# Router logits of the last two token tiles from running sums and eight extra columns of the last second weights, with split second weights kept in DRAM

## Chip, cores and metric

The kernel runs on one core of a Trainium2 chip. The metric is the device time of one execution in microseconds (us), median of three. Below, TensorE, VectorE, ScalarE, GpSimd and SyncE are the engines that the profile calls PE (its weight loads PEld), DVE, ACT, POOL and SP. SyncE issues almost all transfers, from one queue in program order.

## What is computed

Three layers in a row on 1536 tokens (2 sequences of 768) of 512 features. The first is linear attention with a decay, in blocks of 64 tokens. The other two are:

```python
p = domain_probs / (domain_probs.sum(-1, keepdims=True) + 1e-09)   # layer 2, 4 experts, dense
for e in range(4):
    out += p[:, e:e + 1] * (np.maximum(x @ w1[e], 0.0) @ w2[e])    # 512 -> 1024 -> 512
...
logits = x @ w_gate                                                # layer 3, 8 experts, one per token
expert_idx = np.argmax(logits, axis=1)
gate_w = softmax(logits)[expert_idx]
out[mask_e] = gate_w[mask_e, None] * (np.maximum(x[mask_e] @ w1[e], 0.0) @ w2[e])
```

All values are fp32. A product is made of three passes over values split into a high part (`fp32r`) and the rest: high by high, low by high, high by low.

## The kernel before

**Attention and the first pass.** Twelve chunks of 128 tokens go through attention; `warmup` (L1095) runs 54 matmuls on ones ahead of it, `att_a` (L453) multiplies the scores of a chunk by the decays on VectorE, one operation for each half of the heads. The first dense half-expert is worked in between.

**The dense layer.** Tokens come in two sweeps of 768 (6 tiles of 128 each); each sweep goes through 8 half-experts k (512 hidden units). `FAST` passes (k = 1 to 13, `fast_unit`, L714) make the first product of a half-expert in 14 block products ("b phase", line L740, tiles `b`) and then the second product tile by tile ("y phase", `moe1_mm2`, L621, tiles `y`), whose result VectorE adds into `acc` (L636). `hook1(i)` follows block product i, `hook2(j)` follows tile j of the y phase; through them the splits of the next weights (`split_plain`, L184: a copy to the high part on ScalarE, L208, and a subtraction on VectorE, L210) and the router's work are put in order by hand. `KEPT` passes (k = 8 to 13, the second sweep) do not split the first weights `w0` again: the first sweep wrote the parts to DRAM (`kept`, L218), and `kept_steps` loads them. The second weights `w1` are loaded raw and split in every pass. The last dense expert (k = 14 and 15 together, both halves) is done at the end of the sweep, 256 tokens at a time: eight `h` products, then `y` for two tiles. After the f-th `h` of the i-th 256 tokens comes hook 10 i + f, after their tiles hooks 10 i + 8 and 10 i + 9; `plan` lists what is done there.

**The router.** Logits of tiles 0 to 8 are made on VectorE, one operation for each tile and expert (`logit_v`, L845, a product with a row of the router's weights and a sum over 512 values; a ring of five rows is in SBUF). Tiles 9, 10 and 11 use TensorE: four transposes (`route_x`, L853) and a product with the router's weights (`route_lg`, L865). `route_choose` (L875) finds the largest logit (VectorE: `mx`, `sc`, `m2`, `oh` one after the other, and `df`, `seen`), `route_rank` (L915) counts on TensorE how many tokens came before (it reads `oh`), `route_send` makes the row number and scatters the token's row to the expert's bin in DRAM (`scatter`, on GpSimd).

**The end of the dense layer.** The last tiles y = 10 and z = 11 set when the third layer can start. Tile 10 is summed by `moe1_mm2`; tile 11 by `last_dense` (L646) in two halves of 256 columns, each in two runs of 12 matmuls. The transposes and logits of both tiles come between. The first expert's bin is read back (`first_load`, tile `xe`) without the last two tiles; their tokens are put in by a product with a selection matrix (`first_sel`, `first_place`, parts from `first_parts`), on top of the transposed `xe` (`first_T`) in two PSUM banks, two tiles `px` in each. `rows_split` makes the parts `xg` of it, and the products `g` of the first expert begin. `last_sends` scatters the last two tiles; `load_rows` of the first two experts waits for all scatters, and the weights owed to the third layer are loaded behind it.

```python
    y, z = NC - 2, NC - 1
    at(20, route_x, c + 1)          # c + 1 is tile 9, c is tile 8
    at(21, route_choose, c + 1)
    at(23, route_choose, c)
    at(23, route_send, c + 1)
    at(25, route_send, c)
```

Of the kernel before, what the change touches and what calls it, by code (L numbers as in the profile page):

```python
# [18 lines left out]
P = 128  # L19
# [58 lines left out]
def body(ctx: ExitStack, tc: tile.TileContext, lam, att, dp, w1a, w2a, wg, wgt, w1b, w2b, out):  # L78
# [29 lines left out]
    lg_v = const.tile([P, VT, E2], F32, name="lg_v")  # L108
# [32 lines left out]
    loads = [(w, k) for w, k in blocks if w or k not in KEPT]  # L141
    wt = {}
    raws = [rawp]
# [40 lines left out]
    def split_plain(n, c, only=""):  # L184
        b = blocks[n]
        k = b[1]
        if c == 0 and only != "l":
            wt[b] = tuple(
                wp.tile([P, 4, HF], F32R, tag=f"w{b[0]}{x}", name=f"w{b[0]}{x}_{b[1]}")
                for x in "hl"  # L190
            )
        if b in EARLY_AT and c < EARLY:
# [27 lines left out]
    }  # L220

# [231 lines left out]
    def att_a(c):  # L453
# [7 lines left out]
        for r in range(2):  # L461
            V.tensor_tensor(out=a[r], in0=qk[r], in1=w[:, r], op=ALU.mult)
# [179 lines left out]
    def last_parts(hs, j, c, i):  # L642
        return [
            ((hh[:, j * P:j * P + P], hl[:, j * P:j * P + P]),
             tuple(w[:, f % FC, c] for w in wt[1, KL - 1 + f // FC]))
# [3 lines left out]
    def last_dense(hs, t0, j, m, i):  # L649
        t = t0 // P + j  # L650
        c = slice(m * HD, m * HD + HD)
        if i == 0:
            rt["yz"] = ps_mm.tile([P, 512], F32, tag="mm", name=f"yz{m}")[:, :HD]
        ps = rt["yz"]
        mm3(ps, last_parts(hs, j, c, i), i == 0, i == 1)
        if i == 1:
            e = half(KL) // 2
            V.scalar_tensor_tensor(
                out=acc[:, t, c], in0=ps, scalar=p_sb[:, t, e:e + 1], in1=acc[:, t, c],
                op0=ALU.mult, op1=ALU.add,  # L660
            )

# [125 lines left out]
    def open_routing():  # L788
        op = ctx.enter_context(pool("order", 1, side="right"))
        for name, n, d in (  # L790
            ("places", EN, F32), ("caps", EN, F32), ("count", E2, F32), ("place", EN, F32),
            ("cap_e", E2, F32), ("nth", EN, I32), ("tmp", E2 * max(OMAX, E2), F32),
# [59 lines left out]

    def route_x(t, ds=range(KD)):  # L853
# [21 lines left out]
    def route_choose(t):  # L875
        rp = rt["rs"]
        if t < VT:
# [80 lines left out]
    def last_sends():  # L958
# [17 lines left out]
        V.tensor_scalar(  # L976
# [3 lines left out]
        V.tensor_scalar(  # L980
# [3 lines left out]
        V.tensor_tensor(out=at_row, in0=at_row, in1=far, op=ALU.add)  # L984
        V.tensor_tensor(out=pos, in0=at_row, in1=rk_all[:, two], op=ALU.add)
        V.tensor_scalar(out=sums, in0=sums, scalar1=1e-9, scalar2=None, op0=ALU.add)
        V.reciprocal(acc[:, two, DM], sums)
        for i in range(n):
            t = NC - n + i
            scatter(bins, pos[:, i:i + 1], acc[:, t, :], E2 * MOST, "bins")  # L990
# [10 lines left out]
    def first_T(s):  # L1001
        if s == 0:
            px = [ps_mm.tile([P, 512], F32, tag="mm", name=f"px{d}") for d in range(2)]
            rt["px"] = [px[d // 2][:, d % 2 * CAP:d % 2 * CAP + CAP] for d in range(KD)]
        for d in range(KD):
# [860 lines left out]
```

## Time and profile before

| | |
|---|---|
| median of 3 runs | 739.46 us (738.38 to 740.17) |
| the profiled execution's own time | 739.93 us |
| its span, first to last instruction | 738.1 us |
| PE busy | 727.1 us, 99% of the span |
| DVE busy | 510.9 us, 69% |
| ACT busy | 313.7 us, 42% |
| POOL busy | 81.2 us, 11% |
| mean granted TensorE clock | 0.997 |

The span is the stretch in which instructions run; the time is 1.8 us longer. Matmuls are pipelined and the profile models their ends, so a matmul's own duration is longer than its share of the engine, which is the distance between two starts.

### The profile page before, as it was taken

What the parts mean: (1) busy time and instruction counts of PE and PEld (TensorE: products, weight loads), DVE (VectorE), ACT (ScalarE), POOL (GpSimd) and SP (SyncE); (2) the same over time, 40 slices, a digit from 0 to 9 for tenths busy, and PEclk for the clock granted to TensorE, in tenths of its full rate; (3) what the DMA queues carried; (4) which work ended last, traced back from release to release, by engine and by line L of the source; (5) the groups of instructions that cost most, each with busy time, mean ns of one, the idle gap of its engine ahead of it and who ended that gap; (6) DMA issues with size and microseconds to landing.
All of it is one profiled execution on the core that took longest, in us unless ns stands there. A gap on an engine that the chain in (4) does not pass through costs nothing.

```text
span 738.1 us, 12981 instructions
## 1 busy us (share of the span) xinstructions
PE 727.1 (99%) x4951; PEld 658.9 (89%) x4951; DVE 510.9 (69%) x1140; ACT 313.7 (42%) x690; POOL 81.2 (11%) x86
## 2 busy tenths in 40 slices
PE   9999999999999999999999999999999999999995
PEld 8888989889898988989889898988898998998994
DVE  7557776776756766657677667774696867675883
ACT  4333725243342535424223141541153757565772
POOL 3474000000000000000000002100021013121013
PEclk9999999999999999999999999999999999999998
DMA  8763794626446175455161543361143968765661
GB/s 315 286 217 104 249 262 175 256 93 255 158 180 256 58 284 229 155 202 212 59 257 38 218 156 145 100 200 39 52 113 133 323 222 270 255 209 187 229 231 32
DMA packets 39420, 136.79 MB, mean 185 GB/s; under 512 B 6913, under 2 KB 6913, under 8 KB 34747
## 3 DMA queue, kind: packets, MB, share of 16 engines
q1 hardware_dynamic: 37243, 129.63, 50.6%
q0 software_dynamic: 2112, 6.31, 2.2%
q8 instruction: 40, 0.66, 0.4%
q14 instruction: 25, 0.20, 0.1%
HBM read 102.85 MB, written 33.26 MB: 184 GB/s over the span
## 4 chain that ended last, share of the span: by engine, by line
PE 96%; DVE 1%; ACT 1%; issue 1%; POOL 0%; POOLq 0%; DVEq 0%
PE y L595 36%; PE b L740 26%; PE h L595 7%; PE g L595 5%; PE z L595 3%; PE z L1479 3%; PE g L1479 2%; PE zr L1588 2%; PE qk L395 1%; PE z L1480 1%; PE g L1480 1%; PE xo L529 1%; PE zr L1559 1%; PE warm L1098 1%; PE yz L595 1%; PE gr L595 1%
## 5 line engine op out<-in xcount | busy, mean ns | idle before, releaser
L210 DVE TENSOR_TENSOR w1l<-raw,w1h 128x512 fp32r<-128x512 f32 x124 | 82.4, 688 | 28.5 <-ACT w1h L208 28.1
L636 DVE SCALAR_TENSOR_TENSOR acc<-y,p_sb,acc 128x512 f32<-128x512 f32 x77 | 57.8, 751 | 61.2 <-PE y L595 54.2
L747 ACT COPY u<-b 128x384 f32<-128x384 f32 x78 | 36.4, 479 | 108.6 <-PE b L740 107.1
L208 ACT CAST w1h<-raw 128x512 fp32r<-128x512 f32 x124 | 73.1, 619 | 1.1 <-DMA raw<-in_w2a 1.1
L125 POOL DMA_INDIRECT bins<-acc,pos x10 | 11.2, 1117 | 456.9 <-DVE mx L889 378.5
L740 PE MATMUL b<-xh,w0h 128*128 128x384 f32 x208 | 57.8, 339 | 0.0
L210 DVE TENSOR_TENSOR w0l<-raw,w0h 128x512 fp32r<-128x512 f32 x76 | 51.2, 722 | 0.8 <-ACT w0h L208 0.6
L846 DVE CUSTOM_DVE_ANT_0 x<-acc,x 128x512 f32<-128x512 f32 x72 | 49.4, 687 | 1.0
L208 ACT CAST w0h<-raw 128x512 fp32r<-128x512 f32 x76 | 42.9, 623 | 4.5 <-DMA raw<-in_w1a 4.0
L125 POOL DMA_INDIRECT out<-y,xb x16 | 30.0, 1878 | 132.6 <-DVE y L1625 82.8
L754 DVE TENSOR_TENSOR u<-b,u 128x384 f32<-128x384 f32 x78 | 43.1, 552 | 1.4 <-PE b L740 1.4
L740 PEld LDWEIGHTS b<-xh,w0h 128*128 128x128 f32 x208 | 38.2, 188 | 0.6
L595 PE MATMUL g<-xg,w0h 128*128 128x288 f32 (+1 forms) x192 | 38.1, 294 | 0.0
L595 PE MATMUL h<-xh,w0h 128*128 128x256 f32 x144 | 36.0, 292 | 0.2 <-ACT xh L181 0.2
L740 PE MATMUL b<-xl,w0h 128*128 128x384 f32 x104 | 35.2, 339 | 0.0
L595 PE MATMUL h<-xh,w0l 128*128 128x256 f32 x144 | 34.7, 282 | 0.1
L740 PE MATMUL b<-t1h,w0h 128*128 128x384 f32 x104 | 30.8, 337 | 0.0
L595 PEld LDWEIGHTS g<-xg,w0h 128*128 128x128 f32 x192 | 30.8, 188 | 0.0
L740 PE MATMUL b<-xh,w0l 128*128 128x384 f32 x104 | 28.8, 338 | 0.0
L740 PE MATMUL b<-t4h,w0l 128*128 128x384 f32 x104 | 28.8, 337 | 0.0
L740 PE MATMUL b<-t2h,w0l 128*128 128x384 f32 x104 | 28.7, 337 | 0.0
L740 PE MATMUL b<-t3h,w0h 128*128 128x384 f32 x104 | 28.6, 336 | 0.0
(371 smaller groups left out, 2053.6 us busy)
## 6 DMA issues: line engine op xcount, KB each, us to landing
raw<-in_w2a SPq DMA_DIRECT2D x32, 512.0 KB, 3.5
raw<-in_w1b SPq DMA_DIRECT2D x32, 512.0 KB, 5.7
raw<-in_w2b SPq DMA_DIRECT2D x32, 512.0 KB, 4.4
kept<-w0h SPq DMA_DIRECT2D x12, 1024.0 KB, 7.9
w0h<-kept SPq DMA_DIRECT2D x12, 1024.0 KB, 9.5
raw<-in_w1a SPq DMA_DIRECT2D x18, 512.0 KB, 3.7
att<-in_att SPq DMA_DIRECT2D x12, 512.0 KB, 4.7
kept<-w0l SPq DMA_DIRECT2D x6, 1024.0 KB, 6.6
```

The costliest lines, as they stand in the source:

```text
L125: i = G.indirect_dma_start(out=dst, out_offset=bass.IndirectOffsetOnAxis(ap=idx, axis=0), in_=src, in_offset=None, bounds_check=rows - 1, ...
L208: A.copy(out=hi, in_=t)
L210: V.tensor_tensor(out=lo, in0=t, in1=hi.bitcast(F32), op=ALU.subtract)
L595: T.matmul(ps, l, r, start=first and i == 0, stop=last and i == len(ops) - 1)
L636: V.scalar_tensor_tensor(out=acc[:, t, 0:DM], in0=ps, scalar=p_sb[:, t, e:e + 1], in1=acc[:, t, 0:DM], op0=ALU.mult, op1=ALU.add,)
L740: T.matmul(ps, l[:, d, c], r[:, d, :], start=first and i == 0, stop=i == len(ops) - 1, skip_group_check=not first,)
L747: A.copy(out=t, in_=bank[2, s])
L754: V.tensor_tensor(out=t, in0=bank[b, s], in1=t, op=ALU.add)
L846: V.tensor_tensor_reduce(out=x2.rearrange("p d t -> p (d t)")[:, RING * DM:], in0=acc[:, t, 0:DM], in1=logit_piece(e), scale=1.0, scalar=0 ...
L1479: T.matmul(ps[:, :2 * n], wh, both, start=i == 0, stop=False)
L1480: T.matmul(ps[:, :n], wl, hi, start=False, stop=i == len(parts) - 1)
L1588: T.matmul(ps[s][:st], l[:, c], r, start=h == 0 and j == 0, stop=h == 1 and j == len(ops) - 1)
```

## The change

Four things are changed together.

1. The logits of tiles 10 and 11. In the passes k = 10 to 13 VectorE makes, for each of the last dense expert's 1024 rows of second weights, its eight products with the router's rows (`wg_v`, 64 operations on rows loaded anew by `wg_load`, 24 loads of 256 KB); `wg_columns` splits these and puts them behind the 512 columns of the second weights as eight more. `logit_v` is done for tiles 10 and 11 on the sums without the last dense expert, and `last_dense` adds the rest: its right half has 264 columns, and one small VectorE operation adds the last eight to the logits. The transposes and logit products of tiles 10 and 11 go away, and so does `keep_up`.
2. Second weights in the second sweep. In the first sweep the split second weights of passes 2 to 7 are written to DRAM (2 MB each), and passes 8 to 13 load the two parts (`fetch_second`) and split nothing. The order of the router's operations in these passes is denser (`logit`).
3. The end of the dense layer is put in another order: both last tiles by `last_dense`, right half first; tile 8 and 9 are sent one hook earlier; four small operations of `last_sends` move from VectorE to GpSimd; `px` has a bank for each of its four tiles; raw loads of the third layer stand behind `first_load` and not ahead of it.
4. The start: 46 warming matmuls and not 54, and `att_a` of the first two chunks in halves.

```diff
-    loads = [(w, k) for w, k in blocks if w or k not in KEPT]
+    loads = [(w, k) for w, k in blocks if k not in KEPT]
     wt = {}
+    wx = {}
...
+        if c == 3 and b[0] and k < KS and k in kept:
+            for i, t in enumerate(wt[b]):
+                SP.dma_start(out=kept2[k][i], in_=t.bitcast(F32))
...
+    kept2 = {k: dram.tile([2, P, 4, HF], F32, name=f"kept2_{k}") for k in kept}
+    def fetch_second(n, i):
+        k = blocks[n][1]
+        t = wp.tile([P, 4, HF + E2], F32R, tag="w1" + "hl"[i], name=f"w1{'hl'[i]}_{k}")
+        t = t[:, :, :HF]
+        SP.dma_start(out=t.bitcast(F32), in_=kept2[half(k)][i])
+        wt[1, k] = wt.get((1, k), ()) + (t,)
     def pair_of(t, j):
...
-        for r in range(2):
-            V.tensor_tensor(out=a[r], in0=qk[r], in1=w[:, r], op=ALU.mult)
+        step = HP // 2 if c < B else HP
+        for h in range(0, HP, step):
+            for r in range(2):
+                i = slice(h, h + step)
+                V.tensor_tensor(out=a[r][:, i], in0=qk[r][:, i], in1=w[:, r, i], op=ALU.mult)
...
     def last_parts(hs, j, c, i):
         return [
             ((hh[:, j * P:j * P + P], hl[:, j * P:j * P + P]),
-             tuple(w[:, f % FC, c] for w in wt[1, KL - 1 + f // FC]))
+             tuple(w[:, f % FC, c] for w in wx[1, KL - 1 + f // FC]))
...
     def last_dense(hs, t0, j, m, i):
         t = t0 // P + j
-        c = slice(m * HD, m * HD + HD)
+        c = slice(m * HD, m * HD + HD + m * E2)
         if i == 0:
-            rt["yz"] = ps_mm.tile([P, 512], F32, tag="mm", name=f"yz{m}")[:, :HD]
-        ps = rt["yz"]
+            rt["yz"] = ps_mm.tile([P, 512], F32, tag="mm", name=f"yz{j}{m}")
+        ps = rt["yz"][:, :c.stop - c.start]
         mm3(ps, last_parts(hs, j, c, i), i == 0, i == 1)
-        if i == 1:
+        if i == 1 and m:
             e = half(KL) // 2
             V.scalar_tensor_tensor(
-                out=acc[:, t, c], in0=ps, scalar=p_sb[:, t, e:e + 1], in1=acc[:, t, c],
-                op0=ALU.mult, op1=ALU.add,
-            )
+                out=lg_v[:, t, :], in0=ps[:, HD:], scalar=p_sb[:, t, e:e + 1],
+                in1=lg_v[:, t, :], op0=ALU.mult, op1=ALU.add,
+            )
+    def last_sum(t, m):
+        e = half(KL) // 2
+        c = slice(m * HD, m * HD + HD)
+        V.scalar_tensor_tensor(
+            out=acc[:, t, c], in0=rt["yz"][:, :HD], scalar=p_sb[:, t, e:e + 1], in1=acc[:, t, c],
+            op0=ALU.mult, op1=ALU.add,
+        )
     def open_fast():
...
+    def wg_load(u):
+        f = u % (2 * FC)
+        k = half(KL - 1 + f // FC)
+        t = od["wg", u] = st["sf"].tile(
+            [P, 2, HF // 2], F32, tag="sf", name=f"wg{u}").rearrange("p a b -> p (a b)")
+        SP.dma_start(out=t, in_=w2a[k // 2, k % 2, :, f % FC, :])
+    def wg_v(u, e):
+        i = (u % (2 * FC)) * E2 + e
+        V.tensor_tensor_reduce(
+            out=x2.rearrange("p d t -> p (d t)")[:, RING * DM:], in0=od["wg", u],
+            in1=logit_piece(e), scale=1.0, scalar=0.0, op0=ALU.mult, op1=ALU.add,
+            accum_out=od["lw"][:, i:i + 1],
+        )
+    def wg_done(u):
+        if u + 3 < len(TURNS_WG) * 2 * FC:
+            wg_load(u + 3)
+    TURNS_WG = (range(RING, E2), range(E2 - RING, RING), range(E2 - RING))
+    def wg_steps():
+        steps = []
+        for n, es in enumerate(TURNS_WG):
+            for f in range(2 * FC):
+                u = n * 2 * FC + f
+                for e in es:
+                    step = [(wg_v, u, e)]
+                    if e == es[-1]:
+                        step.append((wg_done, u))
+                        if f == 2 * FC - 1 and n != 1:
+                            step += [(logit_load, d + (n and RING)) for d in range(E2 - RING)]
+                    steps.append(step)
+        return steps
+    def wg_columns():
+        lw = od["lw"].rearrange("p (f e) -> p f e", e=E2)
+        for i in range(2):
+            hi, lo = (t[:, :, HF:] for t in wx[1, KL - 1 + i])
+            hi_lo(hi, lo, lw[:, i * FC:i * FC + FC, :])
     def route_x(t, ds=range(KD)):
...
-        V.tensor_scalar(
+        G.tensor_scalar(
...
-        V.tensor_scalar(
+        G.tensor_scalar(
...
-        V.tensor_tensor(out=at_row, in0=at_row, in1=far, op=ALU.add)
-        V.tensor_tensor(out=pos, in0=at_row, in1=rk_all[:, two], op=ALU.add)
+        G.tensor_tensor(out=at_row, in0=at_row, in1=far, op=ALU.add)
+        G.tensor_tensor(out=at_row, in0=at_row, in1=rk_all[:, two], op=ALU.add)
+        G.tensor_copy(out=pos, in_=at_row)
         V.tensor_scalar(out=sums, in0=sums, scalar1=1e-9, scalar2=None, op0=ALU.add)
         V.reciprocal(acc[:, two, DM], sums)
-        for i in range(n):
-            t = NC - n + i
-            scatter(bins, pos[:, i:i + 1], acc[:, t, :], E2 * MOST, "bins")
+        rt["twopos"] = pos
+    def last_scatter(i):
+        scatter(bins, rt["twopos"][:, i:i + 1], acc[:, NC - 2 + i, :], E2 * MOST, "bins")
     def first_load():
...
-    def first_T(s):
-        if s == 0:
-            px = [ps_mm.tile([P, 512], F32, tag="mm", name=f"px{d}") for d in range(2)]
-            rt["px"] = [px[d // 2][:, d % 2 * CAP:d % 2 * CAP + CAP] for d in range(KD)]
-        for d in range(KD):
+    def first_open():
+        px = rt["px"] = {}
+        for d in (2, 3, 0, 1):
+            px[d] = (
+                ps_mm.tile([P, 512], F32, tag="mm", name=f"px{d}") if d != 1 else
+                rt["ps_rt"].tile([P, 512], F32, tag="rtr", name=f"px{d}")
+            )[:, :CAP]
+    def first_T(d):
+        for s in range(NS):
             T.matmul(
                 rt["px"][d][:, s * ST:s * ST + ST], rt["xe"][:ST, s, d * P:d * P + P],
-                ident[:ST, :ST], start=s == 0 and d % 2 == 0, stop=False, is_transpose=True,
+                ident[:ST, :ST], start=s == 0, stop=False, is_transpose=True,
...
-        warmup(warm, 54)
+        warmup(warm, 46)
...
+        y, z = NC - 2, NC - 1
+        for hook, *now in (
+            (1, (y, 3)), (3, (z, 3)), (5, (y, 4)), (6, (z, 4)),
+            (7, (y, 5), (z, 5), (y, 6), (z, 6), (y, 7), (z, 7)),
+            (15, (y, 0)), (16, (z, 0)), (17, (y, 1), (z, 1), (y, 2), (z, 2)),
+        ):
+            for x in now:
+                at(hook, logit_v, *x)
+        at(12, wg_columns)
...
-        at(23, route_send, c + 1)
-        at(25, route_send, c)
+        at(22, route_send, c + 1)
+        at(24, route_send, c)
         logits = []
         for k in FAST:
             def logit(n):
                 for _ in range(n):
-                    if logits:
-                        logit_v(*logits.pop(0))
+                    for what, *args in logits.pop(0) if logits else ():
+                        what(*args)
             def hook1(i):
                 if i % 2 == 0:
                     split_to(1, k)
-                elif KS < k < K1 - 4:
-                    logit(i < 6)
+                elif k in KEPT:
+                    logit((i > 4 or k > KS) + (k == K1 - 4 and i > 12))
...
-                    logit(2 if k == KS else 2 - j % 2)
+                    logit(3 - j % 2 if k < K1 - 4 else 1 - (k > K1 - 4 and j == 5))
...
-                logits = [(t, e) for e in range(E2) for t in range(TT)]
+                for u in range(3):
+                    wg_load(u)
+                logits = [[(logit_v, t, e)] for e in range(E2) for t in range(TT)]
+                logits += wg_steps()
...
+                state["owed"] = 0
                 split_to(0, K1 + 1, 4)
-                state["owed"] = 0
                 split_to(1, K1, EARLY)
                 first_load()
-            for j in range(256 // P - last):
+                while state["load"] < 2 * (loads.index((1, K1 + 1)) + 1):
+                    load_piece()
+                    state["owed"] -= 1
+                break
+            for j in range(256 // P):
                 moe1_mm2(KL, hs, t0, j)
-                if not last:
-                    unit(2 * FC + j)
+                unit(2 * FC + j)
         assert not plan
-        y, z = NC - 2, NC - 1
         low, high = range(KD // 2), range(KD // 2, KD)
-        first_parts(y)
+        low, high = range(KD // 2), range(KD // 2, KD)
+        left, right = slice(0, HD), slice(HD, DM)
+        last_dense(hs, t0, 0, 1, 0)
+        last_dense(hs, t0, 0, 1, 1)
+        route_choose(y)
+        last_sum(y, 1)
+        first_parts(y, right)
+        last_dense(hs, t0, 0, 0, 0)
+        last_dense(hs, t0, 0, 0, 1)
+        last_sum(y, 0)
+        first_parts(y, left)
+        last_dense(hs, t0, 1, 1, 0)
+        route_rank(y)
+        first_sel(y)
+        last_dense(hs, t0, 1, 1, 1)
+        route_choose(z)
+        last_sum(z, 1)
+        first_parts(z, right)
         last_dense(hs, t0, 1, 0, 0)
-        route_x(y)
+        route_rank(z)
         last_dense(hs, t0, 1, 0, 1)
-        last_dense(hs, t0, 1, 1, 0)
-        first_parts(z, slice(0, HD))
-        route_x(z, low)
-        last_dense(hs, t0, 1, 1, 1)
-        route_lg(y)
-        route_x(z, high)
-        route_lg(z, low)
-        first_parts(z, slice(HD, DM), "h")
-        route_lg(z, high)
-        route_choose(y)
-        route_rank(y)
+        first_sel(z)
+        last_sends()
+        last_scatter(0)
+        last_sum(z, 0)
+        last_scatter(1)
+        first_parts(z, left)
+        first_open()
+        for d in (2, 3, 1):
+            first_T(d)
+        first_place(y, high)
+        first_place(z, high)
         first_T(0)
-        first_T(1)
-        first_sel(y)
-        route_choose(z)
+        rt["counts"] = small("counts")[:, :E2]
+        T.matmul(rt["counts"], ones, rt["seen"], start=True, stop=True)
         first_place(y, low)
-        route_rank(z)
-        first_place(y, high)
-        keep_up(1)
-        T.matmul(rt["warm"][:, :E2], ones, rt["seen"], start=True, stop=True)
-        first_sel(z)
-        first_parts(z, slice(HD, DM), "l")
-        first_place(z)
-        last_sends()
+        first_place(z, low)
```

## Rows read from the trace of the kernel before

**Rows 1.** The page: engines' busy time, and the chain that ended last by engine.

```profile
PE 727.1 (99%) x4951; PEld 658.9 (89%) x4951; DVE 510.9 (69%) x1140; ACT 313.7 (42%) x690; POOL 81.2 (11%) x86
...
PE 96%; DVE 1%; ACT 1%; issue 1%; POOL 0%; POOLq 0%; DVEq 0%
```

**Rows 2.** Timeline, 0 to 26 us: start, us, engine, line, operation, [idle before <-releaser].

```profile
0.99 5.75 PE L1098 MATMUL warm<-ones 128*128 128x128 bf16 x54 [0.99 <-POOL ones L1116]
...
6.66 2.06 PE L395 MATMUL qk<-att 64*128 64x128 f32 x32
...
11.90 5.31 DVE L210 TENSOR_TENSOR w0l<-raw,w0h 128x512 fp32r<-128x512 f32 x4
```

**Rows 3.** Timeline of PE at 6.5 us, the last warming matmuls.

```profile
6.40 0.33 PE L1098 MATMUL warm<-ones 128*128 128x128 bf16 x3
```

**Rows 4.** Tile att, 0 to 30 us: its loads, and their time to landing.

```profile
L340 SPq DMA_DIRECT2D att<-in_att x6: 328/374/527, 1.2 to 24.3; - x6
...
DMA to landing us min/median/max: 4.7/7.3/7.4
```

**Rows 5.** Stages, passes 1, 3, 12 and 13: busy by engine, PEclk, DMA share, GB/s.

```profile
78.67:110.21 31.54, 31.54 (x157) 27.99 (x156) 24.34 (x40) 14.80 (x30) 0.53 (x1) 1.00 0.96 293
...
141.75:173.29 31.54, 31.54 (x157) 28.23 (x157) 21.96 (x36) 12.62 (x25) 0.00 (x0) 1.00 0.50 187
...
425.61:457.15 31.54, 31.54 (x161) 27.78 (x160) 21.60 (x75) 9.89 (x26) 2.36 (x3) 1.00 0.45 167
457.15:489.88 32.73, 32.73 (x168) 28.79 (x167) 24.34 (x69) 15.29 (x34) 4.17 (x5) 1.00 0.39 129
```

**Rows 6.** The page's groups: busy, mean ns of one, idle before and releaser.

```profile
L210 DVE TENSOR_TENSOR w1l<-raw,w1h 128x512 fp32r<-128x512 f32 x124 | 82.4, 688 | 28.5 <-ACT w1h L208 28.1
L636 DVE SCALAR_TENSOR_TENSOR acc<-y,p_sb,acc 128x512 f32<-128x512 f32 x77 | 57.8, 751 | 61.2 <-PE y L595 54.2
...
L846 DVE CUSTOM_DVE_ANT_0 x<-acc,x 128x512 f32<-128x512 f32 x72 | 49.4, 687 | 1.0
```

**Rows 7.** Timeline, 530 to 556 us, VectorE's and TensorE's rows around hooks 20 to 27.

```profile
535.58 0.75 DVE L636 SCALAR_TENSOR_TENSOR acc<-y,p_sb,acc 128x512 f32<-128x512 f32 x1 [0.48 <-PE y L595]
...
541.16 0.28 PE L595 MATMUL h<-xh,w0h 128*128 128x256 f32 x1
...
542.14 0.23 DVE L895 TENSOR_SCALAR oh<-sc,m_all 128x8 bf16<-128x8 f32 x1
...
545.08 0.23 DVE L895 TENSOR_SCALAR oh<-sc,m_all 128x8 bf16<-128x8 f32 x1
...
552.95 1.29 DVE L210 TENSOR_TENSOR wel<-raw,weh 128x512 fp32r<-128x512 f32 x2
```

**Rows 8.** The chain that ended last, 548 to 556 us: start, us, engine, line.

```profile
548.81 5.61 PE y L595 x24
554.42 1.43 PE yz L595 x12
```

**Rows 9.** Timeline, 560 to 572 us, around the last tile.

```profile
560.79 0.48 DVE L658 SCALAR_TENSOR_TENSOR acc<-yz,p_sb,acc 128x256 f32<-128x256 f32 x1 [1.67 <-PE yz L595]
...
564.95 0.42 DVE L1021 TENSOR_TENSOR al<-acc,ah 128x256 fp32r<-128x256 f32 x1
...
566.33 0.32 DVE L1419 TENSOR_TENSOR xg<-px,xg 128x176 fp32r<-128x176 f32 x1
566.69 0.52 ACT L1418 CAST xg<-px 128x176 fp32r<-128x176 f32 x2 [0.51 <-DVE xg L1419]
566.69 0.97 POOL L125 DMA_INDIRECT bins<-acc,twopos  x1 [15.55 <-DVE xg L1419]
...
568.39 0.43 PE L1479 MATMUL g<-xg,w0h 128*128 128x352 f32 x1 [0.18 <-DVE xg L1419]
```

**Rows 10.** After the tail: the stage from 569 us, and ScalarE's first wait there.

```profile
569.00:600.00 31.00, 31.00 (x238) 30.99 (x237) 25.62 (x61) 21.37 (x53) 2.44 (x2) 1.00 0.88 296
...
580.10 1.15 ACT L208 CAST w0h<-raw 128x512 fp32r<-128x512 f32 x2 [0.51 <-DMA raw<-in_w1b]
```

More of the change, by code (lines that the diff above doesn't have):

```diff
@@ L107, in body @@
     steps = const.tile([P, OMAX], F32, name="steps")
-    lg_v = const.tile([P, VT, E2], F32, name="lg_v")
+    lg_v = const.tile([P, NC, E2], F32, name="lg_v")
     sent = {"bins": [], "out": []}
@@ L187, in split_plain @@
         if c == 0 and only != "l":
-            wt[b] = tuple(
-                wp.tile([P, 4, HF], F32R, tag=f"w{b[0]}{x}", name=f"w{b[0]}{x}_{b[1]}")
+            wx[b] = tuple(
+                wp.tile([P, 4, HF + E2 * b[0]], F32R, tag=f"w{b[0]}{x}",
+                        name=f"w{b[0]}{x}_{b[1]}")
                 for x in "hl"
             )
+            wt[b] = tuple(t[:, :, :HF] for t in wx[b])
         if b in EARLY_AT and c < EARLY:
@@ L298, in body @@
             steps_q.append((n, None))
+        elif w and k in KEPT:
+            steps_q += [(n, lambda n=n, i=i: fetch_second(n, i)) for i in range(2)]
         else:
@@ L791, in open_routing @@
             ("places", EN, F32), ("caps", EN, F32), ("count", E2, F32), ("place", EN, F32),
[L792 removed]
+            ("cap_e", E2, F32), ("lw", 2 * FC * E2, F32), ("nth", EN, I32), ("tmp", E2 * max(OMAX, E2), F32),
         ):
@@ L876, in route_choose @@
         rp = rt["rs"]
-        if t < VT:
+        if t < VT or t >= NC - 2:
             lg = lg_v[:, t, :]
@@ L1045, in route_order @@
         by_pair = od["tmp"][:, :EN * EN].rearrange("p (a b) -> p a b", a=EN)
-        sm = rt["warm"][:, :E2]
+        sm = rt["counts"]
         key = rt["rp"].tile([P, EN], F32, tag="key", name="key", bufs=1)
@@ L1098, in warmup @@
             T.matmul(ps[:, :P], ones, ones, start=True, stop=True)
-    def keep_up(n):
-        rt["warm"] = small("warm_rt")
-        warmup(rt["warm"], n)
     with tc.manual_schedule():
@@ L1421, in body @@
         xg = {0: rows_tiles(0)}
-        for d in range(KD):
+        for d in (2, 3, 0, 1):
             rows_split(xg[0][0][:, d, :], xg[0][1][:, d, :], rt["px"][d])
@@ L1493, in moe2_mm1 @@
                 ((wh[:, d, c:c + P], wl[:, d, c:c + P]),
-                 (hi[:, d, :], lo[:, d, :], both[:, d, :])) for d in range(KD)
+                 (hi[:, d, :], lo[:, d, :], both[:, d, :]))
+                for d in (range(KD) if e else (2, 3, 0, 1))
             ])
@@ L1522, in moe2_mm1_rows @@
                     hook(h * KD + d)
-            g = st["gt"].tile([P, HF], F32, tag="gr", name=f"gr{e}_{h}")
+            g = st["gt"].tile([P, HF], F32, tag="gr", name=f"gr{e}_{h}", bufs=1)
             A.activation(out=g[:n], in_=ps[:n], func=AF.Relu)
@@ L1766, in body @@
                 SP.dma_start(out=xb, in_=rest[bass.ds(i * P, P), :])
-                ws = [[wp.tile([P, 4, HF], F32, tag=f"w{w}{x}", name=f"o{w}{x}")
-                       for x in "hl"] for w in (0, 1)]
+                ws = [[wp.tile([P, 4, HF + E2 * w], F32, tag=f"w{w}{x}", name=f"o{w}{x}")
+                       [:, :, :HF] for x in "hl"] for w in (0, 1)]
                 for w, src in enumerate((w1b, w2b)):
```

## The prediction

> **What bounds the kernel now.** The page is read first: TensorE is busy for 99% of the span, and the chain that ended last is TensorE's own for 96% [rows 1]. So time comes only from work that leaves TensorE's queue, from the few places where it waits, or from new waits put in front of it. The chain in order of time shows where it is broken: at the start, where warming matmuls hold the queue [rows 2], and between the last dense tile and the third layer [rows 8, 9]. The stages of the passes between show TensorE busy for the whole of each pass, with VectorE at 70 to 76% [rows 5]; there the change can only cost. VectorE's free time in the passes is mostly spent waiting for a finished tile y [rows 6], that is, it runs behind TensorE and holds nobody up. The reader should see in the timeline of the end that this turns round: VectorE waits for a tile at 535.58, and from there it works nearly without a break until the last split at 554.24 [rows 7].
>
> **The start.** The warming matmuls take 5.75 us for 54, 0.107 each, until the last three, which are shorter and start 0.055 apart from 6.40 on [rows 2, 3]: 128 columns in 0.107 is the 1.2 GHz level, in 0.055 the 2.4 GHz level, though PEclk reads 1.00 for all of it. Forty-six end at 0.99 + 46 x 0.107 = 5.91. The first `att` is issued at 1.2 and lands at the earliest 4.7 later, at 5.9 [rows 4], so `qk` can begin at about 5.9. Up to 6.40 it runs at half speed and does 0.25 us worth of work; against 6.66 now [rows 2] TensorE is then 0.47 us ahead. Bounds: 0, if what comes next sets the pace, and 8 x 0.107 = 0.86. Next in line is VectorE with four subtractions in 5.31 us, 1.3 each where the same form takes 0.69 elsewhere [rows 2, 6]; they are fed by `xl`, which moves forward with TensorE, so I take 0.47. `att_a` in halves turns four operations into eight and lets the first begin on half of the scores; a gain and a loss of some 0.4 each are possible, and I count it at nothing.
>
> The Trainium skill (TensorE: Matmul & The Clock Gate, What's actually happening) says that activity lifts the clock and that the point moves from run to run. By that, eight matmuls fewer don't bring 6.40 forward, which is how the sum above is made; by a count of matmuls it would be 0.86 us instead of 0.47.
>
> **First sweep.** Passes 2 to 7 write 2.1 MB more each. Pass 3 moves 187 GB/s x 31.54 us = 5.9 MB; with 2.1 more it is 8.0 MB, 254 GB/s. Pass 1 moved 293 GB/s and TensorE was busy throughout [rows 5]. The stores stand behind the split that they wait for, where SyncE waits anyway. Cost 0; without that cover raw weights would come late, bound 1 us.
>
> **Second sweep.** In each of passes 8 to 13 four subtractions go (4 x 0.69 = 2.75 us of VectorE) and their copies on ScalarE; loads grow by 1 MB of parts and up to 1.9 MB of rows for `wg_v`, to about 8.2 MB a pass, again below pass 1. Products of logits rise from 12 to 20 or 22 a pass in 8 to 11, and from none to 14 and 12 in passes 12 and 13, at 0.69 each [rows 6]. Pass 12: 21.60 - 2.75 + 14 x 0.69 = 28.5 of 31.54. Pass 13: 24.34 - 2.75 + 12 x 0.69 = 29.9 of 32.73 [rows 5]. So VectorE fills up to 91%, yet a tile's bank is needed only three tiles later, so it may fall a few us behind. Cost 0; without cover, what exceeds the pass, 1 to 4 us (a rival). The 16 products for tiles 10 and 11 stand at hooks 1 to 17, where VectorE catches up before 535.58 (it has 0.48 to spare there [rows 7], and more before); cost 0, bound 0.5.
>
> **Tiles 8 and 9 sent one hook earlier.** This is a cost. The rank is a matmul in TensorE's queue, and it reads `oh`. For tile 9 `oh` is done at 542.37; now its rank follows the fourth `h`, which starts at 541.16 [rows 7]. Moved one hook up it stands ahead of that `h`, and TensorE waits 542.43 - 541.16 = 1.3 us. VectorE can't be earlier: since 535.58 it has done one thing after another. Then tile 8: its `oh` is done at 545.31 now, before the send of tile 9. In the new order the send (six small operations, about 1.0 us by the 0.23 of such a one) comes first, so `oh` is done near 546.4, while TensorE arrives after two `h` of 1.43 (twelve matmuls of 256 columns, as in [rows 8]) at 545.4: another 1.1 us. TensorE ends the `h` at about 551.1, not 548.7, and behind it VectorE's relu and six splits end at 555.5 to 556, not 554.24. What waits behind the rank is every `h` product, and for those ScalarE and VectorE.
>
> **The end.** Removed are 8 transposes, 8 logit products and the idle time among them, now between 554.42 and 568.39 [rows 8, 9]. In the new order I walk both queues forward from the numbers above.
> TensorE: tiles 10 and 11 are eight runs of 12 matmuls, each 1.43 as now [rows 8], four of them 3% wider: 11.6 us, so 562.7 without a wait, and about 563.1 with that for the rank of tile 11. Transposes and the placements of the right half come to about 1.5 more, up to 564.6 (14 at an estimated 0.1, since 256 columns take 1.43 / 12 = 0.12); the last placements need the parts of tile 11's left half.
> VectorE: from 555.8, for tile 10 the logits (0.25), the choice (1.0), two sums of 0.48, two subtractions of 0.42, about 0.45 each time in which it waits for ScalarE's copy between them (an estimate from the 0.42 and 0.48 of the same 256 columns), and the selection (0.5): 4.4 us. For tile 11 the same and the two ranks with sums (0.6): 5.1. The last part is done at 565.4 [rows 9]. So VectorE, not TensorE, sets the end.
> Then four splits into `xg`. Now ScalarE's copies wait for VectorE's subtractions of the same bank, 0.51 once, and four take from 566.33 to about 568.3 [rows 9]. With a bank for each, two are ready while the last parts are made, and four subtractions of 0.32 to 0.34 with the last placements between them put the fourth group of the first `g` at 566.9, where it is at 568.39 now: 1.5 us earlier. Bounds: without the two waits it would be 565.5 (2.9 us), without any wait for VectorE about 563.4 (5.0 us); no gain at all, if the four small GpSimd operations or the later reads take it back. GpSimd's operations are off TensorE's path; for them, the nearest row is the scatter, 0.97, so four cost at most 4 us, which the scatter at 566.69 [rows 9] would feel, and the row loads behind it.
>
> **Sum.** 0.47 + 1.5 = 2.0 us of the profiled execution's 739.93: 737.9. That execution stood 0.47 above the median of 739.46, so the median to expect is 737.5.
>
> **Rivals.**
> A. The two ranks don't wait, because VectorE comes to them earlier than I have it. For it: it has slack before 535.58. Against: it is held there by the tile itself [rows 7]. 739.46 - 0.47 - 2.9 = 736.1, or down to 734 if it is also quicker at the end.
> B. Slower: VectorE, or the rows for `wg_v`, don't keep up in passes 10 to 13. The rows queue behind up to 3.5 MB of `w0` parts in the y phase, and a late row stops VectorE, the sums and then the banks. For it: 91% of a pass. Against: TensorE has three banks of time. It decides when it costs over 0.9 us in each of the four passes (2.0 gained, 1.5 to be seen): 4 x 1 gives 741.5; 4 x 0.5 gives 739.5.
> C. The end's gain is given back in the third layer. From 569 us the transfers are at 88%, and ScalarE waits 0.51 us for a raw weight at 580.10 [rows 10]. If weights and rows are no earlier, only the start is left: 739.0. Against: TensorE is busy for all of that stage in spite of the wait, and the scatters move forward with the end.
> D. The switch to 2.4 GHz comes later than 6.40, with shorter warming, and `qk` and `xo` run at half speed: the start's gain is lost, 738.0; a stretch of 2 us more would make it 739.
> The Trainium skill's rule above bears on D: the point is run-variable; one profile can't show that.
>
> **How the numbers follow.** As forecast (both gains, both waits), 736.0 to 738.7: 0.48. A: 0.15. B: 0.14, two thirds of it slower by over 0.2%. C: 0.13. D: 0.10. The range from 734.2 (part of A beyond it) to 740.4 (the light half of B within it) leaves out about 0.17. A measurement here can tell 0.2%, 1.5 us: faster is below 738.0. Most of the forecast, all of A and some of D make 0.57; the rest of the forecast, C, most of D and the light part of B make 0.33; slower 0.10.
>
> **What would show it.** Right: in the changed profile the first `qk` starts at 5.9 to 6.0; passes 1 to 13 take 31.54 each; TensorE's queue waits 1.3 and 1.1 us for `oh` at hooks 22 and 24; from VectorE's wait for the tile at 535.58 to the fourth group of the first `g` it is 1.5 us shorter than 568.39 - 535.58 = 32.8 us. Wrong: a pass longer than 31.6, a wait for `w1` parts or a `wg` row in front of VectorE, no wait at the ranks, or the stage from the first `g` to the last matmul longer than now.

## The result, and the profile after

The changed kernel takes 744.87 us (median of six runs, 742.75 to 747.22), the kernel before 738.75 in the same runs: ratio 1.008, 95% interval 1.0067 to 1.0092. It is slower by 6.1 us, where 2.0 less was forecast, and outside the range of 734.2 to 740.4.

The profiled execution is the fastest of the six: 742.75, span 741.0 (before 739.93 and 738.1). Of the page, the line of the engines and two groups:

```profile
PE 723.7 (98%) x4942; PEld 656.8 (89%) x4942; DVE 544.4 (73%) x1282; ACT 300.0 (40%) x666; POOL 81.4 (11%) x91
...
L656 DVE SCALAR_TENSOR_TENSOR acc<-y,p_sb,acc 128x512 f32<-128x512 f32 x76 | 56.9, 749 | 31.5 <-PE y L615 30.2
...
L890 DVE CUSTOM_DVE_ANT_0 x<-wg,x 128x512 f32<-128x512 f32 x64 | 43.9, 686 | 6.1 <-DMA wg<-in_w2a 5.4
```

TensorE works 3.4 us less than before and the span is 2.9 longer: it waits more [rows 1]. VectorE's idle time in front of the sums, its reserve, fell from 61.2 to 31.5 [rows 6], and a new wait has come, 5.4 us for the rows `wg`. Windows of the changed kernel, passes 3, 8, 11, 12 and 13 (columns as in [rows 5]):

```profile
140.09:171.68 31.59, 31.59 (x158) 28.31 (x156) 22.07 (x36) 12.60 (x25) 0.00 (x0) 1.00 0.68 253
...
297.92:331.77 33.85, 32.06 (x158) 28.19 (x157) 23.20 (x58) 10.17 (x19) 0.00 (x0) 1.00 0.79 280
...
394.88:426.46 31.58, 31.58 (x157) 28.32 (x156) 22.56 (x57) 6.74 (x14) 0.00 (x0) 1.00 0.77 270
426.46:461.83 35.37, 32.74 (x164) 28.15 (x163) 29.54 (x104) 7.67 (x22) 2.18 (x2) 1.00 0.63 231
461.83:493.86 32.03, 32.03 (x163) 28.38 (x162) 27.76 (x92) 13.28 (x30) 4.57 (x5) 1.00 0.52 176
```

Two passes stand out: pass 8 is 2.3 us longer and pass 12 3.3, cut at the first `b` of each pass as here (the kernel before has 31.54 and 32.05). In both, TensorE is busy for less than the window. What it waited for, over the whole span (us in total, times, longest):

```profile
PE rank L987 <- DVE oh L964: 2.4, 3, 1.1
PE y L615 <- DMA w1l<-kept: 1.4, 1, 1.4
PE b L768 <- ACT u L775: 1.4, 1, 1.4
PE rank L987 <- DVE rk_all L1004: 1.2, 3, 0.8
...
PE y L615 <- DMA w1h<-kept: 0.4, 1, 0.4
```

The `w1` waits are pass 8's, and `b` for `u` and the ranks for `rk_all` are pass 12's; the `oh` waits stand behind the passes, at the sends of tiles 8 and 9, and were forecast. Pass 8 is read from SyncE's timeline:

```profile
299.76 2.24 SPq L869 DMA_DIRECT2D x<-in_wgt  x5
302.05 1.38 SPq L886 DMA_DIRECT2D wg<-in_w2a  x3
303.47 0.87 SPq L234 DMA_DIRECT2D w1h<-kept  x1
304.39 1.48 SPq L234 DMA_DIRECT2D w1l<-kept  x1
...
417.83 0.38 SPq L304 DMA_DIRECT2D w0l<-kept  x1
418.50 7.20 SPq L886 DMA_DIRECT2D wg<-in_w2a  x3
```

The parts of the second weights go out at 303.47, behind eight rows of 256 KB, and `y` wants them 14.8 us into the pass, at 312.7; the three `wg` rows among the eight are first read at 381.5, in pass 10. The last two lines are pass 11: rows behind `w0` parts. What that does is in the timeline of the whole core at the change from pass 11 to 12:

```profile
423.38 0.69 DVE L890 CUSTOM_DVE_ANT_0 x<-wg,x 128x512 f32<-128x512 f32 x1 [2.90 <-DMA wg<-in_w2a]
...
427.81 0.69 DVE L890 CUSTOM_DVE_ANT_0 x<-wg,x 128x512 f32<-128x512 f32 x1 [2.46 <-DMA wg<-in_w2a]
...
433.90 0.55 DVE L782 TENSOR_TENSOR u<-b,u 128x384 f32<-128x384 f32 x1
...
434.49 0.52 ACT L622 ACTIVATE ht_000h<-u 128x384 fp32r<-128x384 f32 x1 [5.18 <-DVE u L782]
...
435.43 0.44 PE L768 MATMUL b<-t3h,w0h 128*128 128x384 f32 x1 [1.41 <-ACT u L775]
```

VectorE stands for 2.90 and 2.46 us before late rows. From 427.81 it works through its order without a break and comes to the first `u` of pass 12 only at 433.90; ScalarE has then waited 5.18 for that `u`; its next copies of the banks stand behind this operation in its queue, and TensorE, which needs such a bank, waits 1.41. The ranks of pass 12 then wait for the same late engine.

The start and the end, from the timeline of the changed kernel:

```profile
0.97 4.16 PE L1174 MATMUL warm<-ones 128*128 128x128 bf16 x46 [0.97 <-POOL ones L1187]
5.97 2.44 PE L412 MATMUL qk<-att 64*128 64x128 f32 x32 [0.84 <-DMA att<-in_att]
...
540.22 0.75 DVE L656 SCALAR_TENSOR_TENSOR acc<-y,p_sb,acc 128x512 f32<-128x512 f32 x1 [0.52 <-PE y L615]
547.08 0.17 PE L987 MATMUL rank<-oh,upper 128*128 128x8 bf16 x1 [1.12 <-DVE oh L964]
551.31 0.17 PE L987 MATMUL rank<-oh,upper 128*128 128x8 bf16 x1 [1.06 <-DVE oh L964]
571.34 0.36 PE L1573 MATMUL g<-xg,w0h 128*128 128x352 f32 x1
```

The balance of the two profiles, in us after less before: start to the first `b` (78.51, now 76.86) -1.7 (1.8 by the cut of [rows 5], as two expectations below have it); passes 1 to 13 +5.8; from there to VectorE's wait for the tile +0.5; from that wait to the fourth group of the first `g` (32.81, now 31.12) -1.7; the rest 0. That makes the 2.9 of the spans. The 6.1 between the medians is more, and the start is too good; both are taken up below.

### The profile page after: what moved, and what is told of

Its sections match the earlier page's. It is cut to its first block, busy times and chain, and to the rows that moved or that the text cites. A ratio compares the mean times of both kernels' runs of the same rounds, so it can differ in the third digit from the quotient of the medians.

```text
span 741.0 us, 13156 instructions
## 1 busy us (share of the span) xinstructions
PE 723.7 (98%) x4942; PEld 656.8 (89%) x4942; DVE 544.4 (73%) x1282; ACT 300.0 (40%) x666; POOL 81.4 (11%) x91
## 5 line engine op out<-in xcount | busy, mean ns | idle before, releaser
L656 DVE SCALAR_TENSOR_TENSOR acc<-y,p_sb,acc 128x512 f32<-128x512 f32 x76 | 56.9, 749 | 31.5 <-PE y L615 30.2
L213 DVE TENSOR_TENSOR w1l<-raw,w1h 128x512 fp32r<-128x512 f32 x100 | 65.7, 685 | 15.3 <-ACT w1h L211 13.9
L874 DVE CUSTOM_DVE_ANT_0 x<-acc,x 128x512 f32<-128x512 f32 x88 | 60.5, 688 | 1.7
L211 ACT CAST w1h<-raw 128x512 fp32r<-128x512 f32 x100 | 58.2, 618 | 1.5 <-DMA raw<-in_w2a 1.5
L890 DVE CUSTOM_DVE_ANT_0 x<-wg,x 128x512 f32<-128x512 f32 x64 | 43.9, 686 | 6.1 <-DMA wg<-in_w2a 5.4
```

Source lines behind the costliest of these rows:

```text
L211: A.copy(out=hi, in_=t)
L213: V.tensor_tensor(out=lo, in0=t, in1=hi.bitcast(F32), op=ALU.subtract)
L656: V.scalar_tensor_tensor(out=acc[:, t, 0:DM], in0=ps, scalar=p_sb[:, t, e:e + 1], in1=acc[:, t, 0:DM], op0=ALU.mult, op1=ALU.add,)
L874: V.tensor_tensor_reduce(out=x2.rearrange("p d t -> p (d t)")[:, RING * DM:], in0=acc[:, t, 0:DM], in1=logit_piece(e), scale=1.0, scalar=0 ...
L890: V.tensor_tensor_reduce(out=x2.rearrange("p d t -> p (d t)")[:, RING * DM:], in0=od["wg", u], in1=logit_piece(e), scale=1.0, scalar=0.0, ...
```

## The experiments

Theory 1: row loads and loads of parts get in each other's way, in pass 8 the parts behind the rows, in pass 11 the rows behind the parts, and VectorE has no room for what it loses by it. Rivals: VectorE has too many operations whatever the loads do; the parts, twice the bytes of the raw weights, are the loss by themselves; the loss is of one queue's order and not of the sixteen DMA engines. Lengths of passes from first `b` to first `b` of the profiled execution, VectorE's waits for rows in passes 10 to 13, and the medians:

| run | pass 8 | pass 12 | waits for rows | us | ratio, 95% |
|---|---|---|---|---|---|
| changed kernel | 33.85 | 35.37 | 5.4 | 744.87 | 1.0080 (1.0067 to 1.0092) |
| e13, the same again | 34.36 | 37.08 | 7.1 | 746.05 | one run |
| e1, rows from GpSimd's queue | 31.54 | 37.36 | 7.7 | 745.48 | 1.0084 (1.0067 to 1.0101) |
| e2, parts of pass 8 ahead | 31.54 | 35.89 | 5.9 | 741.15 | 1.0027 (1.0015 to 1.0038) |
| e3, three rows loaded once | 35.94 | 32.25 | 0 | - | - |
| e4, no products, no rows | 31.54 | 32.05 | - | - | - |
| e6, two turns | 34.40 | 32.27 | 0 | 741.15 | 1.0038 (1.0024 to 1.0052) |
| e7, e2 and e6 | 31.53 | 32.25 | 0 | 738.01 | 0.9990 (0.9981 to 1.0000) |
| e8, e7 with late sends | 31.54 | 32.26 | 0 | 736.29 | 0.9967 (0.9955 to 0.9980) |

Pass 12 of e1, e2 and e13 and pass 8 of e3 hold 1.7 us each of a lower granted clock behind a wait (see e13).

**e1: another queue for the rows.**

```diff
 def wg_load(u):
-        SP.dma_start(out=t, in_=w2a[k // 2, k % 2, :, f % FC, :])
+        G.dma_start(out=t, in_=w2a[k // 2, k % 2, :, f % FC, :])
```

> The 24 loads of rows of the last second weights (wg, L886) are issued from GpSimd's queue in place of SyncE's; nothing else is changed. Changed kernel: 744.87 (ratio 1.008), in its profile pass 8 33.85, pass 12 35.37, VectorE's waits for those rows 2.90 and 2.46. Theory 1 (rows and parts stand behind each other on one queue; VectorE loses 5.4 waiting for rows that stand behind the stored parts and starts pass 12 late): the two waits fall under 1 in all, pass 12 is 32.0 to 32.5, the w1 parts of pass 8 go out 1.4 earlier and pass 8 is about 32.5; 740.5, ratio 1.002. Rival a (VectorE is simply full in passes 11 and 12): pass 12 stays over 35, only pass 8 gains, 743.5, ratio 1.006. Rival b (the sixteen DMA engines, not the queue, are full when the rows are asked for): the waits stay near 5, 743.5.

Pass 8 is mended, pass 12 is worse, the total the same. The tile `wg` in this run:

```profile
L886 POOL DMA_DIRECT2D wg<-in_w2a x24: 536/538/784, 261.2 to 472.0; - x24
...
  DVE x L890: 7.7, 6
...
DMA to landing us min/median/max: 2.9/5.9/9.1
```

With a queue of their own the rows still take 5.9 us in the middle and up to 9.1 to land. Rival b holds for pass 12: the DMA engines are full, with a busy share of 0.96 to 1.04 in every 2 us from 416 to 428 (in e8, where no row is late, 0.44 and 0.00 from 420 to 424). The Trainium skill (DMA: Bandwidth & Descriptors, Issuing engines are not separate DMA queues) says that transfers run on the same sixteen engines and interleave, whichever engine started them; these landings agree. That the order in SyncE's queue has no part in it is not shown: without the rows there, the `w1` parts of pass 12 (2 MB), which the changed kernel issues at 433.66, go out at 414.04 and fill the same stretch.

**e2: the parts of pass 8 first.**

```diff
 if k == KS - 1:
+                split_to(1, KS, 2)
                 for e in range(RING):
                     logit_load(e)
```

> At the change of sweep the two loads of the w1 parts of pass 8 are issued ahead of the five rows of the router's weights and the three rows of the last second weights instead of behind them; nothing else is changed. Theory 1: they go out some 4 us earlier, the waits of TensorE for w1l and w1h (1.4 and 0.4) are gone, pass 8 is 31.6 in place of 33.85, pass 12 stays near 35.4; 742.6, ratio 1.005. Rival (the parts are not late because of what stands ahead of them but because their bytes, 2 MB beside the w0 parts, don't land in the 15 us of the first half of the pass whatever the order): pass 8 over 33, 744.5, ratio 1.008.

As theory 1 has it, pass 8 is 31.54 and the wait gone; the total fell by 3.7, more than the 2.3 of the profile. With the old order the loss in pass 8 differs from execution to execution: 2.3 in the changed kernel's first profile, 2.8 in e13, 2.9 in e6 and 4.4 in e3.

**e3 and e4: the rows and the operations apart.**

```diff
 def wg_done(u):                                   # e3
-        if u + 3 < len(TURNS_WG) * 2 * FC:
-            wg_load(u + 3)
+        od["wg", u + 3] = od["wg", u]
...
-                    step = [(wg_v, u, e)]         # e4
+                    step = []
...
```

> Only the first three rows of the last second weights are loaded; all 64 products of VectorE are kept and take these three in turn (so the logits of the last two tiles lack most of the last expert's part). Same VectorE work, 21 loads of 256 KB less. Theory 1: no wait of VectorE for a row, pass 12 32.0 to 32.3, pass 8 as before (its three rows still stand ahead of the w1 parts) 33.9; 741.6, ratio 1.004. Rival a (the number of VectorE operations is what does not fit): pass 12 stays over 35 and the total at 744.9, ratio 1.008.

> The 64 products and the 24 row loads are left out and the eight columns are zero (the logits of the last two tiles lack the last expert's part); the stored second weights, the new end and the rest stay. 47 us less of VectorE in passes 10 to 13. Theory 1: pass 12 as before the change, 32.0; the w1 parts of pass 8 still stand behind the five router rows but not behind three more, pass 8 32.5; 740.3, ratio 1.002. Rival c (loading the second weights as stored parts, twice the bytes, is the loss by itself): pass 8 33.85 and other passes over 31.6 too, 743 or more.

Their totals (807.56 and 828.21) say nothing here: with other logits the tokens of the last two tiles go to other experts, and the loop for rows beyond an expert's places runs, for which TensorE waits 44.7 and 55.8 us. All that stands before the last tiles is unharmed. Windows of e3, passes 8 and 12:

```profile
297.87:333.81 35.94, 33.60 (x157) 29.33 (x156) 23.22 (x58) 10.16 (x19) 0.00 (x0) 0.95 0.82 288
428.51:460.76 32.25, 32.20 (x165) 28.15 (x163) 26.63 (x97) 7.94 (x22) 2.18 (x2) 1.00 0.56 207
```

and of e4:

```profile
297.84:329.38 31.54, 31.54 (x158) 28.33 (x156) 23.22 (x58) 10.18 (x19) 0.00 (x0) 1.00 0.71 250
424.08:456.13 32.05, 32.05 (x164) 28.06 (x163) 18.48 (x69) 7.94 (x22) 2.99 (x3) 1.00 0.52 197
```

e3 has every product and nearly no loads for them: pass 12 is 32.25. So the count of VectorE's operations fits, and the waits for rows are what didn't. Pass 8 in e3 keeps its loss, for its three rows are still loaded first; it is even longer than in the changed kernel, since behind the waits for the parts (0.92 and 1.42 us) the granted clock fell to 0.50. e4 has the parts and no rows: both passes are as before the change, pass 8 even with the five rows of the router ahead of the parts. That is better than expected (32.5): the three `wg` rows alone tip it over.

**e6 and e7: fewer loads for the same products.**

```diff
-    TURNS_WG = (range(RING, E2), range(E2 - RING, RING), range(E2 - RING))
+    TURNS_WG = ((*range(RING, E2), *range(E2 - RING, RING)), range(E2 - RING))
...
-                        if f == 2 * FC - 1 and n != 1:
-                            step += [(logit_load, d + (n and RING)) for d in range(E2 - RING)]
+                    if f == 2 * FC - 1 and e in (E2 - 1, E2 - RING - 1):
+                        step += [(logit_load, d + (n and RING)) for d in range(E2 - RING)]
```

> The 64 products go in two turns over the eight rows (experts 5, 6, 7, 3, 4, then 0, 1, 2) in place of three, so each row is loaded twice, not three times: 16 row loads, 5 or 3 products from each row, the same number of VectorE operations, ring of three rows as before. Theory 1 as the first four runs left it (VectorE has no room in passes 10 to 13 for the 5 to 8 us that it loses to rows which land late behind the stored parts, and the number of operations itself fits): the waits for rows fall from 5.4 to under 2, pass 12 32.0 to 33 in place of 35.4; pass 8 as in the changed kernel, 33.9; 741.5, ratio 1.004. Rival (rows come as late as before whatever their number, since the stored parts fill the DMA engines after each pass): waits over 4, pass 12 over 35, 744.9.

> Both: the w1 parts of pass 8 ahead of the rows, and the two turns. Theory 1: pass 8 31.6, pass 12 32.0 to 33; from the run with the parts ahead alone (741.15, pass 12 35.9 with TensorE at the low clock for 4 us) 3 to 4 less: 737.6, ratio 0.998, under the kernel before. Rival: as with the parts ahead alone, 741.2, ratio 1.003.

A row now serves five or three products, not three or two, so a late one is asked for earlier relative to its use, and a third of the loads is gone. The edit also moves the three router rows of pass 11: the changed kernel issues them at 415.40, right ahead of the `w0` parts and the late rows, e6 at 427.40, behind these parts. No run tells the two effects apart. The waits vanish and pass 12 is 32.27; with the parts ahead as well both passes are mended, and TensorE has no wait left in passes 8 to 13. Windows of e7, passes 8 and 12:

```profile
297.87:329.40 31.53, 31.53 (x157) 28.33 (x156) 23.24 (x58) 10.19 (x19) 0.00 (x0) 1.00 0.65 222
...
424.11:456.36 32.25, 32.20 (x165) 28.14 (x163) 26.64 (x97) 7.94 (x22) 2.18 (x2) 1.00 0.70 249
```

Against the kernel before in the same runs, 6.1 more (744.87 against 738.75) has become 0.6 less (738.01 against 738.59): the two places explain 6.7 us, all of the loss.

**e8: the sends back where they were.** `at(22, route_send, c + 1)` and `at(24, route_send, c)` become 23 and 25 again.

> The kernel with both, and the sends of tiles 9 and 8 back at hooks 23 and 25. If the two waits of TensorE at the ranks (1.12 and 1.06) are a loss that the later hook takes away: 2.2 less than the kernel with both, near 735.4. Rival (the rows of the last two tiles then reach the first rows of the experts later, or the ranks wait elsewhere): within 0.5 of the kernel with both.

1.7 less than e7 and 0.33% under the kernel before: the fastest of all, with e12. The timeline of e8, with the waits at these two ranks gone:

```profile
535.01 0.75 DVE L656 SCALAR_TENSOR_TENSOR acc<-y,p_sb,acc 128x512 f32<-128x512 f32 x1 [0.51 <-PE y L615]
542.03 0.18 PE L987 MATMUL rank<-oh,upper 128*128 128x8 bf16 x1
545.06 0.18 PE L987 MATMUL rank<-oh,upper 128*128 128x8 bf16 x1
564.44 0.35 PE L1574 MATMUL g<-xg,w0h 128*128 128x352 f32 x1
```

From VectorE's wait to the fourth group of the first `g` it is 29.43, against 31.12 and, before, 32.81 [rows 7, 9]. Of the 2.2 expected, a part comes back at the rank of tile 11, which now waits 0.67 for `oh` (559.20).

**e9, e10 and e12: the start.** e9 is e7 with 54 warmups; e10 the kernel before with 46 warmups and the weighing in halves; e12 is e8 with the weighing whole.

> The kernel with both, with 54 warmups as before the change; the att halves of the weighing stay. By the forecast the eight fewer were worth 0.4 to 0.5 at the first qk; the measured start was 1.8 shorter. If the warmups make it: time to the first b 1.5 to 1.8 later than in the kernel with both (76.7), 739; if the halves of the weighing make it: under 0.5 later.

> The kernel before with the start of the change alone: 46 warmups in place of 54 and the weighing of the first chunks in halves of the heads. By the forecast (first qk 0.5 earlier, all of it kept) 0.5 less: ratio 0.9994; by the changed kernel's profile (first b 1.8 earlier) 1.8 less: ratio 0.9976; if the two profiles differed by their executions and not by the edit, within 0.3.

> The kernel with w1 parts ahead, two turns and late sends (736.29), with the weighing of whole chunks as before the change; 46 warmups. If the halves are what brings the first xo forward: the two whole products hold xo back by about the 0.2 to 0.9 that the earlier profiles show there, 736.5 to 737.2; if xo waits for neither: 736.3.

e9: 738.25 (e7: 738.01). e10: 738.70, ratio 0.9996 (0.9987 to 1.0005). e12: 736.30 (e8: 736.29). Neither the warmups nor the halves make a difference that the medians show. In the profiles the first `b` is at 77.87 in e9 (e7: 76.81) and at 76.88 in e10 (before: 78.51). Both profiled executions lose elsewhere: in e10 the granted clock falls to 0.50 at 566 to 569, so that it takes 739.52 in spite of its start; in e9, with 741.89 the longest of its eleven, TensorE waits 1.65 for rows of the bins in the third layer, and the clock falls behind that.

**e11: the stored second weights alone**, put into the kernel before.

```diff
-    loads = [(w, k) for w, k in blocks if w or k not in KEPT]
+    loads = [(w, k) for w, k in blocks if k not in KEPT]
...
+        elif w and k in KEPT:
+            steps_q += [(n, lambda n=n, i=i: fetch_second(n, i)) for i in range(2)]
```

> The kernel before with the stored second weights of passes 8 to 13 alone (stored in passes 0 to 5, loaded as high and low parts in place of split). Theory 1 (the loading by itself is hidden, only together with the rows did it come late): every pass as before, 31.4 to 31.6 and 32.0, total within 0.5 of the kernel before, ratio 0.9993 to 1.0007. Rival c (twice the bytes are a loss by themselves, at the change of sweep above all): pass 8 over 32.5, ratio 1.0015 or more.

738.61, ratio 0.9997 (0.9988 to 1.0006), passes 8 and 12 at 31.55 and 32.05: rival c falls. This run also shows what the start of a profile is worth. It has 54 warmups, as before:

```profile
0.99 4.75 PE L1111 MATMUL warm<-ones 128*128 128x128 bf16 x54 [0.99 <-POOL ones L1129]
6.00 2.46 PE L408 MATMUL qk<-att 64*128 64x128 f32 x32 [0.27 <-DMA att<-in_att]
```

They take 4.75 us, not 5.75 [rows 2], `qk` starts at 6.00 and the first `b` at 76.95. In this execution the 2.4 GHz level came some 2 us earlier (the matmuls start 0.055 apart from 4.34 on, not from 6.40), and the start is as short as that of the changed kernel.

**e13: the changed kernel again.**

> The changed kernel once more, for a second profiled execution: the first took 742.75, the five others 744.07 to 747.22. If the granted clock makes that spread (as after the waits of 1.9 and 3.4 us in the runs with the parts ahead and with GpSimd's queue): an execution of 744 to 747 shows, right behind the wait in pass 8 or in pass 12, some 4 us at 0.5 of full clock, 2 us lost for each such place, and passes 1 to 7 and 9 to 11 at 31.5 to 31.7. If something else makes it, the clock stays at 1.00 there and the time is lost elsewhere.

An execution of 746.05. VectorE waited 4.67 and 2.42 us for rows, TensorE 3.1 for `u`. Windows of 2 us around that wait:

```profile
436.00:438.00 2.00, 0.00 (x0) 0.00 (x0) 1.41 (x4) 0.92 (x3) 0.00 (x0) 1.00 0.60 146
438.00:440.00 2.00, 1.98 (x8) 1.98 (x9) 1.41 (x5) 1.02 (x3) 0.00 (x0) 0.66 0.82 302
440.00:442.00 2.00, 2.00 (x8) 2.00 (x7) 1.97 (x6) 0.56 (x2) 0.00 (x0) 0.50 1.04 390
442.00:444.00 2.00, 2.00 (x13) 2.00 (x12) 1.26 (x3) 0.89 (x3) 0.00 (x0) 0.98 1.05 399
```

Column seven is the granted clock: behind the wait TensorE works at 1.2 GHz for 3 to 4 us, 8 matmuls in 2 us and not 13; the shares below 1.00 add up to some 1.7 us lost. In the first profile, behind 1.41 us, it did not fall:

```profile
436.00:438.00 2.00, 2.00 (x13) 2.00 (x12) 1.41 (x5) 1.04 (x3) 0.00 (x0) 1.00 0.95 351
```

Of the 3.3 us between these two executions, pass 12 has 1.7 and pass 8 0.5, so in these two most of the difference is made there; the other executions of the spread of 742.75 to 747.22 have no profile.

## Why the prediction was wrong

**The step that failed: "Second sweep ... Cost 0".** It compared sums: bytes of a pass with those of pass 1, VectorE's busy time with the length of a pass. Both sums hold (e3, e11, and passes 9 to 11 at 31.6). What was missing is when a load goes out and what stands beside it. Cost measured: 2.3 us in pass 8 and 3.3 in pass 12 in the best execution, 6.7 in the medians (e7). Without this cost e7 is 0.6 under the kernel before, not 2.0: the start's share doesn't show in the medians.

**"A tile's bank is needed only three tiles later."** True in the y phase, where VectorE was late in pass 11 and TensorE didn't wait. But what VectorE owes at the end of that phase it still owes when the `b` products begin, and there TensorE needs its banks back in the order of `u`. The reserve was read from the wrong phase.

**Rival B** had the mechanism of pass 12, rows behind up to 3.5 MB of `w0` parts, with too small a chance (0.14) and a wrong condition: not 0.9 us in each of four passes, but 3.3 to 5.0 in one. Pass 8, the parts of the second weights behind rows, was priced in no case, though a wait for `w1` parts stands among the signs of being wrong; each DMA of the new order had not been followed past the others at the change of sweep.

**The start: 0.47 forecast** (0.51 by its own terms: 6.66 - 6.40 and 0.25), with `qk` at 5.9 to 6.0 (measured 5.97). The gain can't be told from nothing (e10: -0.5 us by the medians, interval of both signs). The profile of before was one of a late switch to 2.4 GHz; e11 reaches 6.00 with all 54. The forecast's choice to hold the switch still at 6.40 was wrong: it is the execution's, not the kernel's. The Trainium skill (TensorE: Matmul & The Clock Gate, What's actually happening) says that this point moves from run to run, and the two runs with 54 warmups agree. What the eight matmuls are worth hangs on it, as far as single profiles tell: with the early level `qk` waits for `att` either way, and the first `b` is at 76.86 with 46 and 76.95 with 54 (e11); with the late one it is at 76.88 with 46 (e10, where they take 5.08 us) and at 78.51 and 77.87 with 54 (before, e9). So that `qk` came at 5.97 as forecast doesn't show the forecast's reason, and in the changed kernel the level came early, at 4.02, so D's case was not met.

**First sweep: cost 0** was right: pass 3 moved 253 GB/s (254 forecast) in 31.59.

**The ranks** waited 1.12 and 1.06 (1.3 and 1.1 forecast), so rival A falls; taking these waits away gave 1.7 in the medians.

**The end** was 1.7 shorter (1.5 forecast). **The third layer** gave nothing back (169.7 in both profiles), so rival C falls for the changed kernel. With the passes mended it shows a little: e7 and e8 have 170.3 and 170.1 there, with waits of 0.7 and 0.3 for rows of the bins.

**Two readings of [rows 5]** were off without changing the sum: VectorE is busy for 68 to 77% of these passes, not 70 to 76%, and "passes 1 to 13 take 31.54 each" doesn't hold in the kernel before either; cut at the first `b`, its passes 12 and 13 are 32.05 and 31.95.

**Left open:** the stretch from the last pass to VectorE's wait for the tile is 0.5 longer (in e8 too). Some 0.3 of it lies in the first eight `h` products of the last expert (11.86 us, 11.52 before) and some 0.3 ahead of the rank at 534.31, which waits 0.18 for `oh`; why is open.

## What to carry to other kernels

A sum of bytes or of busy time that fits a stage doesn't say that a load lands in time: follow each new load past what is issued ahead of it and what fills the DMA engines when it goes out, and ask how many operations of its reader cover that. When an engine is filled to over 80% in a fixed order (VectorE with 26.6 of 32.25 us in pass 12 of e7), a wait of a few us has no place to go, and it shows where that engine next owes something to the bound one, maybe in the phase after. Loads that are first used late belong behind those that are used soon, and using a loaded row for more operations can cost less than another queue for it.

## What the runs showed of the hardware

Short waits of TensorE can cost more than themselves. Behind 1.9 us (e2, pass 12), 3.1 us (e13), 3.4 us (e1), 1.65 us (e9) and the pair of 0.92 and 1.42 us in pass 8 of e3 its granted clock fell to 0.5, and each fall lost 1.7 us by the shares below 1.00, which nearly doubled the price of the first. The length of a wait alone doesn't tell whether it falls: behind 0.90 and 1.43 us in pass 8 of e6, and behind 1.41 us in the changed kernel, it stayed at 1.00, while in e10 it fell at 566 behind 0.48 and 0.20 us, waits that stand in the kernel before too (0.49 and 0.21 at 566.71 and 567.42), without a fall in its profile.

And the same 54 warming matmuls took 5.75 us in one execution and 4.75 in another, and the first `b` of the two came 1.6 us apart (78.51 and 76.95).
